# A 2-D real FFT filter pair with a gated mix: a new order list, with some steps on other engines

## The chip, the cores and the metric

The kernel runs on one core of a Trainium2 chip. The metric is the device time of one execution in microseconds, as the median of several runs. The core has five engines that each work through their own queue in order: TensorE (PE; its weight loads, PEld, overlap its matmuls), VectorE (DVE), ScalarE (ACT), GpSimd (POOL) and SyncE (SP), which here only issues transfers. They meet through semaphores.

## The reference

```python
def _A_ref(x, w_r, w_i):                 # _B_ref is the same
    B, S, D = x.shape                    # 1, 2048, 1024
    X = rfft2(x.astype(float32), axes=(-2, -1))
    X = X * (w_r + 1j * w_i)             # w_r, w_i: 2048 x 513
    return irfft2(X, s=(S, D), axes=(-2, -1)).astype(bfloat16)

x = A_x
g = sigmoid((x * gate_w).sum(-1, keepdims=True))
return g * _A_ref(x, A_w_r, A_w_i) + (1 - g) * _B_ref(x, B_w_r, B_w_i)
```

Both filters act on the same x (B_x is not used), so the forward transform is made once, the products and inverse transforms twice, and the gate mixes the two results row by row. All inputs are bfloat16.

## The kernel before

Every transform is a matmul with a constant matrix. Rows are split as 2048 = 128 × 16 (s2, s1), columns into four quarters, so that even and odd frequencies (parity e and o) can be treated apart. `ORDER` is one long list of tokens; the program executes the list in order, and each token emits its instructions on one engine. So each engine's queue is the order of its tokens, and nothing else is scheduled. The letter at the end of a token names the engine (A, D, P for ScalarE, VectorE, GpSimd), the digit at the end of a TensorE token its PSUM bank.

The stages, with their tokens:

- **Loading.** `x:S:s:n` loads n of the 16 blocks of x, `c` constants, `W:S:n` the weights of unit n (16 units: 0 to 7 even, 8 to 15 odd), all issued by SP except the F1 constants and the gate weights `gws` (ScalarE). At most eight transfers are in flight: each further issue waits for the eighth before it. `warm` runs eight matmuls on zeros, `tab` loads ScalarE's sigmoid table.
- **Column transform.** `F1:s1:par` (line 321) makes eight matmuls of 128 columns into one bank. Its two halves are added and subtracted into the tile y: either one half is copied out (`FC`) and VectorE folds the copy with the bank (`FD`, two instructions), or both halves are copied (`FX`) and GpSimd folds (`FP`). `pw` and `gc` prepare small weights on GpSimd.
- **Row transform.** For each unit, `F2` (four matmuls for each of two halves), its copy `T`, `F3` (12 matmuls with the twiddles WF and their negated imaginary part WN) and its copy `X`. `neg` makes WN from WF on ScalarE.
- **Products.** `P:n:r` (line 488) multiplies X with four weight planes, 128x2048 elements for each r, on VectorE; `Y` on TensorE, `NA` and `N` on VectorE patch one column of the product.
- **Inverse row transform.** `J` (32 matmuls) into two times two banks, its two copies `R` (128x1024 each) into a ring of five `rl` buffers, two stores `H` to a scratch in HBM. When all 16 stores of a parity have landed, `L:par:v` loads them back in another layout, eight loads of 512 KB: the even ones over x, the odd ones over weights.
- **Gate.** `GH`, `GC`, `GT`, `GK`, `GZ` form the gate from y, `GS` applies the sigmoid (two instructions), `GW` (line 436) multiplies the inverse matrix E with it into EA and subtracts that from E into EB, for four s1 at a time.
- **Inverse column transform and output.** `V` (eight matmuls with EA and EB, which also mixes the two filters) and its copy `VC`; then, for each v and s, matmuls with IG: `C` keeps the cosine and sine half apart (four matmuls of 256 columns), `U` gives their sum (four of 512). An even row is made from `C`: whole (`E`), or copied out and mixed on GpSimd (`EX`, `EQ`), or its sine half copied and both sums made on VectorE (`ES`, `EF`: in the code, unused). An odd row adds to and subtracts from the even row: on VectorE from PSUM (`OR`), or copied out (`OC`) and mixed by GpSimd (`OP`), or through a buffer (`QD`, `QP`). `S` stores the result.

The copies' scratch `tmp` is a rotation of eight tiles in wx, which later holds the weights of units 8 to 11.

Of the kernel before, what the change touches and what calls it, by code (L numbers as in the profile page):

```python
# [712 lines left out]
```

## Time and profile before

| | us |
|---|---|
| time, median of 3 runs | 117.29 (117.25 to 117.5) |
| span of the profiled execution | 115.6 |
| VectorE busy | 97.0 |
| TensorE busy | 103.6 |
| ScalarE busy | 84.4 |
| GpSimd busy | 46.2 |
| bytes moved, mean rate | 36.79 MB, 318 GB/s |

The span is what the page of the profile covers, from the first to the last instruction of one execution; the time also holds what lies around it. Busy TensorE time includes the drain of each matmul, so it is not TensorE at its peak. A row of a group names the line, the engine, the operation, output and input tile with their shapes, the count, and then busy time, mean length of one and idle time before it. A row of the chain of waits or of a timeline begins with its start and its length in microseconds.

### The profile page before, as it was taken

To read this page: it belongs to the slowest core of one execution; us is meant where nothing else is said; L and a number is where in the kernel's file an instruction comes from. 1 tells how busy PE (TensorE), PEld (TensorE's weight loads), DVE (VectorE), ACT (ScalarE), POOL (GpSimd) and SP (SyncE) were. 2 spreads that over 40 slices of the span, in tenths; PEclk is the share of its full clock that TensorE was granted. 3 is DMA by queue.
4 is the path that set the end of the run, shared out by engine and by line. 5 is a ranking of instruction groups with operands and counts; after the bars stand their busy time and mean duration, and the time that the engine had idled before them with its cause. 6 is when DMAs were issued, how large, how long until landed. Compare 5 with 4: busy or idle time off the path is not lost.

```text
span 115.6 us, 3953 instructions
## 1 busy us (share of the span) xinstructions
PE 103.6 (90%) x1619; PEld 71.3 (62%) x1619; DVE 97.0 (84%) x164; ACT 84.4 (73%) x138; POOL 46.2 (40%) x74
## 2 busy tenths in 40 slices
PE   5999999999999699898889899989979999999900
PEld 2499989875567256463445357459859765867400
DVE  0099999999999999999899999999157349999970
ACT  4009488999999999999999999977735844534300
POOL 1066995900000000000000000057986999999920
PEclk9999999999999999999999999999999999999995
DMA  3999999999579999669999999999999992482874
GB/s 90 348 326 401 403 374 367 363 397 408 210 222 324 371 394 373 169 263 397 350 293 354 348 306 401 254 357 382 352 353 411 403 418 98 198 346 119 327 279 181
DMA packets 17794, 36.79 MB, mean 318 GB/s; under 512 B 1904, under 2 KB 10736, under 8 KB 17776
## 3 DMA queue, kind: packets, MB, share of 16 engines
q1 hardware_dynamic: 17488, 36.44, 87.5%
q8 instruction: 12, 0.20, 0.6%
q10 hardware_dynamic: 288, 0.10, 0.4%
q14 instruction: 6, 0.05, 0.1%
HBM read 23.96 MB, written 12.58 MB: 316 GB/s over the span
## 4 chain that ended last, share of the span: by engine, by line
PE 39%; DVE 19%; DMA 16%; ACT 16%; issue 4%; SPq 1%; DVEq 1%; ACTq 0%
ACT rl L204 11%; PE ps L581 9%; PE ps L565 8%; DVE y L382 7%; PE ps L450 6%; PE ps L334 5%; DMA sc<-rl 5%; DMA re<-sc 4%; DMA ig<-cst_ig 4%; PE ps L537 3%; DMA re<-in_x_dram 3%; PE ps L480 3%; DVE p L494 3%; ACT X L204 3%; PE ps L590 3%
## 5 line engine op out<-in xcount | busy, mean ns | idle before, releaser
L615 POOL TENSOR_TENSOR re<-wx 128x256 f32<-128x256 f32 x28 | 19.6, 730 | 55.3 <-DMA re<-sc 53.1
L204 ACT CAST rl<-ps 128x1024 bf16<-128x1024 f32 x29 | 29.6, 1142 | 0.7 <-ACT wx L204 0.7
L204 ACT COPY wx<-ps 128x256 f32<-128x256 f32 (+1 forms) x39 | 17.2, 498 | 10.5 <-PE ps L334 8.2
L537 PE MATMUL ps<-p,wj 32*64 32x512 bf16 x512 | 20.5, 381 | 2.5 <-ACT rl L204 2.0
L204 ACT CAST V<-ps 128x512 bf16<-128x512 f32 x25 | 13.8, 601 | 11.3 <-PE ps L565 8.4
L494 DVE TENSOR_TENSOR p<-X,ro 128x2048 bf16<-128x2048 bf16 x16 | 19.1, 1215 | 0.0
L450 PE MATMUL ps<-fd,y 128*128 128x256 bf16 x128 | 16.5, 273 | 0.4 <-ACT rl L204 0.4
L382 DVE TENSOR_TENSOR y<-ps,wx 128x256 bf16<-128x256 f32 x48 | 16.4, 412 | 0.1
L334 PEld LDWEIGHTS <-re 128*128 128x128 bf16 x256 | 15.2, 100 | 1.6 <-DMA re<-in_x_dram 1.0
L334 PE MATMUL ps<-f,re 128*128 128x128 bf16 x256 | 15.8, 224 | 0.3
L204 ACT CAST T<-ps 128x512 bf16<-128x512 f32 x26 | 15.5, 693 | 0.0
L537 PEld LDWEIGHTS <-wj 32*64 32x64 bf16 x512 | 8.4, 103 | 10.6 <-issue 7.5
L382 POOL TENSOR_TENSOR y<-wx 128x256 bf16<-128x256 f32 x16 | 11.1, 734 | 8.2 <-DVE wx L206 5.9
L635 DVE TENSOR_TENSOR ot<-re,ps 128x512 bf16<-128x512 f32 x22 | 13.8, 681 | 0.4
L450 PEld LDWEIGHTS <-y 128*128 128x128 bf16 x128 | 11.5, 97 | 4.1 <-issue 2.6
L581 PE MATMUL ps<-ig,V 128*128 128x512 bf16 x56 | 13.4, 380 | 0.0
L204 ACT CAST X<-ps 128x1024 bf16<-128x1024 f32 x12 | 13.2, 1118 | 0.0
L206 DVE COPY wx<-ps 128x512 f32<-128x512 f32 (+1 forms) x10 | 5.8, 578 | 7.4 <-PE ps L334 4.8
L480 PE MATMUL ps<-T,wf 64*64 64x256 bf16 (+1 forms) x128 | 10.2, 332 | 1.1 <-DVE np L514 1.0
L590 PE MATMUL ps<-ig,V 128*128 128x256 bf16 x72 | 9.7, 273 | 0.0
L494 DVE TENSOR_TENSOR p<-X,wx 128x2048 bf16<-128x2048 bf16 x8 | 9.4, 1217 | 0.0
L494 DVE TENSOR_TENSOR p<-X,y 128x2048 bf16<-128x2048 bf16 x8 | 9.3, 1215 | 0.0
(60 smaller groups left out, 138.4 us busy)
## 6 DMA issues: line engine op xcount, KB each, us to landing
sc<-rl SPq DMA_DIRECT2D x32, 256.0 KB, 4.7
ro<-in_we_dram SPq DMA_DIRECT2D x8, 512.0 KB, 8.3
re<-sc SPq DMA_DIRECT2D x8, 512.0 KB, 6.1
ro<-sc SPq DMA_DIRECT2D x8, 512.0 KB, 7.7
re<-in_x_dram SPq DMA_DIRECT2D x7, 512.0 KB, 8.0
out_dram<-ot SPq DMA_DIRECT2D x7, 512.0 KB, 2.6
wx<-in_wo_dram SPq DMA_DIRECT2D x4, 512.0 KB, 6.6
y<-in_wo_dram SPq DMA_DIRECT2D x4, 512.0 KB, 5.0
```

What stands on the lines that cost most here:

```text
L204: nc.scalar.copy(out=out, in_=in_)
L334: nc.tensor.matmul(o, lhsT=lh, rhs=rh, start=(h == 0), stop=(h == 1))
L382: Q[e].tensor_tensor(yo[:, v, k:k + n, s1, :], a.rearrange("p (k c) -> p k c", c=4), b.rearrange("p (k c) -> p k c", c=4), op)
L450: nc.tensor.matmul(ps[:, v * 256:v * 256 + 256], lhsT=y[:, v, par, b, 2 * t:2 * t + 2, :, :].rearrange("p j s c -> p (j s c)"), rhs=C["FD" ...
L480: nc.tensor.matmul(view(ps[ho, tt * 512:(tt + 1) * 512], dst), lhsT=lh, rhs=view(T[hp(jh), tt, :], src), start=(w == 0), stop=(w == 1))
L494: nc.vector.tensor_tensor(p[:, r], xb, w, ALU.mult)
L537: nc.tensor.matmul(o, lhsT=lh, rhs=src[r, ri, wi, tt], start=(q == 0), stop=(q == 3))
L565: nc.tensor.matmul(ps[:, ch * 128:ch * 128 + 128], lhsT=RR[par][:, v, ch // 2, s, c0 + 256 * ab:c0 + 256 * ab + 128], rhs=Ew[:, s1, :], st ...
L581: nc.tensor.matmul(ps, lhsT=Vs[par, v][:, s, ch, :], rhs=rh, start=(ch == 0), stop=(ch == 3))
L590: nc.tensor.matmul(ps[:, o:o + 256], lhsT=Vs[par, v][:, s, ch, :], rhs=g[:, o:o + 256], start=(ch % 2 == 0), stop=(ch % 2 == 1))
L615: Q[e].tensor_tensor(EV[:, v, s, 256 * h:256 * h + 256], t[:, 0], t[:, 1], (ALU.add, ALU.subtract)[h])
L635: nc.vector.tensor_tensor(otile(v)[:, s, h, :], EV[:, v, s], PS["O", 1, v, s], (ALU.add, ALU.subtract)[h])
```

## The change

The order list is replaced. By tokens, before and after:

| | before | after |
|---|---|---|
| folds: `FD` VectorE / `FP` GpSimd / whole row `FG` | 24 / 8 / 0 | 20 / 11 / 1 |
| `T` on VectorE / ScalarE | 6 / 26 | 7 / 25 |
| `X` | 4 / 12 | 3 / 13 |
| `R` | 3 / 29 | 5 / 27 |
| `VC` | 7 / 25 | 4 / 28 |
| gate tiles `GW` (two instructions each) | 4 VectorE | 4 GpSimd |
| even rows whole / mixed by `EQ` / by `EF` | 2 / 14 / 0 | 0 / 6 / 10 |
| `EQ` on GpSimd / VectorE | 28 / 0 | 9 / 3 |
| odd rows as `U` / as `C` | 14 / 2 | 10 / 6 |
| `OR` / `OP` / `QD`, `QP` / `OF` | 22 / 6 / 4, 4 / 0 | 20 / 12 / 0 / 6 |
| result stores | 9 | 13 |

Other parts: x is loaded in another order of blocks (4, 10, 2, 8, 14, 6, 0, 1, 12) with `w0` second, and F1's blocks follow it; F1's constants are issued by ScalarE behind `gws` and `tab`; the constants FD, WF, WJ, PM come behind all of x, EZ, E and IG later. The negated twiddles are a third block of the constant WF, so `neg` and WN are gone and WF has 576 KB in its second load instead of 384. The sine copy of `ES` has a scratch tile of its own for each row, and a new pair does for odd rows what `ES` and `EF` do for even ones: `OS` copies the sine half, `OF` makes sum and difference on VectorE into a scratch tile, from which GpSimd's `OP` makes the two output halves.

```diff
-warm:8 c:A:F1 c:A:gws tab:A x:S:0:1 x:S:1:1 x:S:2:2 x:S:4:2 x:S:6:2 x:S:8:2 x:S:10:2 x:S:12:2 x:S:14:2 c:S:FD:0:1
-F1:1:o:0 F1:1:e:1 FX:1:o:D F1:0:o:2 FC:1:e:D F1:0:e:3 FP:1:o FD:1:e F1:3:o:0 F1:2:e:4 FC:0:e:D F1:3:e:1 gc:P FD:0:e
-F1:2:o:5 FC:3:e:A FC:2:e:D F1:4:e:3 FD:3:e FX:2:o:A F1:5:o:6 FX:0:o:A FD:2:e F1:5:e:5 FC:4:e:A FP:0:o FX:3:o:A FD:4:e
...
-OR:5:1:1 U:1:7:0:4 VC:1:7:1:A EQ:7:1:1:P OR:5:1:0 V:1:6:0:0 QP:3:1:1:P OR:7:0:0 S:S:5 U:1:7:1:1 VC:1:6:0:A OR:7:0:1
-VC:1:6:1:A QP:3:1:0:P U:1:6:0:0 S:S:7:0 OR:7:1:1 OR:7:1:0 U:1:6:1:2 QP:3:0:1:P OR:6:0:0 S:S:7:1 OR:6:1:1 OR:6:0:1
-S:S:3 OR:6:1:0 S:S:6
+warm:8 c:A:gws tab:A c:A:F1 x:S:4:2 c:S:w0 F1:5:e:1 x:S:10:2 F1:4:o:3 x:S:2:2 pw:P F1:10:o:6 F1:10:e:4 FC:5:e:A FD:5:e gc:P
+FC:4:o:A F1:11:o:2 FX:10:o:A x:S:8:2 FC:11:o:A F1:3:e:7 FP:10:o x:S:14:2 F1:11:e:5 FD:4:o F1:3:o:3 FX:10:e:D F1:4:e:1 x:S:6:2
+x:S:0:1 F1:2:e:6 FC:3:e:A FC:11:e:A FC:4:e:A F1:8:e:4 FX:3:o:A x:S:1:1 FD:11:o FP:10:e FD:11:e F1:9:o:5 FC:8:e:A FD:3:e
+F1:9:e:0 x:S:12:2 FX:2:e:A FD:4:e FC:9:e:A F1:8:o:7 c:S:WF:0:4 FC:9:o:A FP:3:o F1:14:e:2 FP:2:e F1:15:e:6 c:S:PM c:S:WJ:0:4
+c:S:FD:0:1 FC:8:o:A FX:14:e:A FD:8:e FD:9:e F1:7:e:3 FD:9:o F1:6:e:4 FC:6:e:A F1:0:e:5 FD:8:o F1:0:o:2 FP:14:e FD:6:e
+F1:1:e:7 F1:12:e:1 FC:7:e:A FX:15:e:A FC:0:e:A FX:1:e:A FD:7:e FD:0:e F1:2:o:6 F1:13:e:4 FP:15:e FC:12:e:A F1:12:o:0 F1:5:o:5
+FX:2:o:A FP:1:e FD:12:e FC:13:e:A F1:14:o:3 F1:15:o:6 FX:0:o:A FD:13:e F2:1:0:2 FC:5:o:A FX:14:o:A FC:15:o:A F2:1:1:1
+FC:12:o:D W:S:0 c:S:FD:1:2 T:1:0:A FD:5:o W:S:1 T:1:1:A FD:12:o F2:0:0:3 F1:13:o:7 T:0:0:A F2:0:1:5 F3:1:1 F2:2:1:3 FC:13:o:A
+FD:15:o T:0:1:A F3:0:5 X:1:A FP:2:o F2:2:0:4 W:S:3 c:S:WF:4:16 FD:13:o F2:3:0:2 T:2:1:D P:1:0 X:0:A Y:1:3 F2:3:1:7 NA:1:D
+T:3:0:A FG:1:o:6 T:3:1:A P:1:1 P:0:0 F1:6:o:3 W:S:5 W:S:2 T:2:0:A FY:1:o:A F3:3:0 c:S:EZ c:S:E FP:0:o FX:6:o:A Y:0:4 P:0:1
+X:3:A F1:7:o:7 FP:14:o FP:6:o NA:0:D F2:5:1:5 N:1:D T:5:1:A W:S:9 c:S:WJ:4:16 W:S:4 FC:7:o:D F2:5:0:6 N:0:D F3:2:2 FD:7:o
+T:5:0:A X:2:A F2:4:0:4 J:1:0:5 F2:4:1:7 Y:2:2 T:4:0:A GH:3 R:1:0:A R:1:1:A T:4:1:A P:3:0 GC:A J:0:5:0 W:S:11 P:2:0 Y:3:7
+NA:2:D W:S:7 F3:5:2 P:2:1 H:1:0 W:S:6 P:3:1 F2:6:0:4 NA:3:D N:2:D R:0:0:A GT:0:7 R:0:1:A X:5:D GT:3:7 N:3:D GT:1:7 GT:2:7
+P:5:0 F3:4:5 GK:A T:6:0:A X:4:A J:2:2:0 F2:6:1:7 Y:5:6 P:5:1 R:2:1:A H:0:1 H:1:1 H:2:1 GZ:0:4 T:6:1:A NA:5:D GS:0 R:2:0:D
+P:4:0 Y:4:6 F3:6:0 NA:4:D GZ:1:2 X:6:A GS:1 F2:7:0:4 F2:7:1:5 T:7:1:A P:4:1 T:7:0:D J:3:0:6 R:3:0:A R:3:1:D F2:8:1:2 F2:8:0:5
+Y:6:4 F3:7:0 N:4:D W:S:10 N:5:D T:8:1:A J:4:2:6 NA:6:D P:6:0 P:6:1 T:8:0:A X:7:A W:S:8 P:7:0 R:4:0:A W:S:15 H:3:0 H:2:0
+J:5:0:4 F2:9:1:3 F2:9:0:2 N:6:D T:9:1:D R:4:1:A T:9:0:D P:7:1 F3:8:6 R:5:0:A F2:11:0:3 R:5:1:A X:8:A H:3:1 J:6:4:0 P:8:0
+Y:7:6 NA:7:D H:4:0 W:S:12 W:S:13 F2:11:1:7 T:11:1:D T:11:0:A P:8:1 F3:9:2 R:6:0:A c:S:IG H:5:0 R:6:1:A F2:10:1:7 F3:11:5
+X:9:A H:4:1 H:5:1 T:10:1:A N:7:D W:S:14 J:8:0:3 F2:10:0:2 X:11:A P:9:0 H:6:1 R:8:0:D R:8:1:A F2:12:1:6 F2:12:0:7 P:11:0
+T:10:0:A H:0:0 T:12:1:A H:8:1 J:7:4:0 T:12:0:A R:7:0:A F3:10:2 P:9:1 J:9:6:4 R:7:1:A F2:13:0:0 R:9:0:A X:10:D R:9:1:A
+F2:14:1:2 F2:14:0:3 F3:12:6 H:6:0 P:11:1 P:10:0 F2:15:1:5 T:14:1:D T:14:0:A F2:13:1:1 P:10:1 X:12:A H:7:0 F3:14:2 T:15:1:A
+J:10:6:4 T:13:0:D T:13:1:A GW:P:4:4 H:8:0 P:12:0 X:14:A H:7:1 P:12:1 F3:13:0 R:10:0:A GW:P:0:4 L:0:3 F2:15:0:3 R:10:1:A
+X:13:A T:15:0:A L:0:1 V:0:3:1:2 J:11:6:4 VC:0:3:1:D P:14:0 L:0:4 L:0:6 L:0:0 H:9:0 V:0:1:1:1 V:0:3:0:0 P:14:1 R:11:0:A H:10:0
+L:0:2 VC:0:1:1:A VC:0:3:0:D P:13:0 R:11:1:A J:12:6:2 R:12:0:D R:12:1:A J:14:0:4 P:13:1 H:10:1 H:11:0 F3:15:2 X:15:D V:0:1:0:6
+GW:P:12:4 R:14:0:A C:0:3:1:7 V:0:0:1:1 P:15:0 R:14:1:A VC:0:1:0:A C:0:3:0:0 V:0:0:0:4 VC:0:0:1:A EX:3:0:A H:12:1 H:9:1
+J:13:2:5 GW:P:8:4 C:0:0:1:0 EX:3:1:D H:14:1 VC:0:0:0:A EQ:3:0:0:P H:11:1 C:0:0:0:4 V:0:2:1:7 R:13:0:A EX:0:1:D R:13:1:A
+EQ:3:0:1:P EX:0:0:D P:15:1 EQ:3:1:0:D C:0:1:1:1 EQ:0:0:1:D EX:1:1:A VC:0:2:1:D C:0:1:0:0 EX:1:0:A V:0:4:0:4 V:0:2:0:3
+J:15:5:1 L:0:5 VC:0:4:0:A H:12:0 V:0:5:1:4 VC:0:2:0:A EQ:3:1:1:P L:0:7 C:0:2:1:0 R:15:0:A EQ:0:0:0:P V:0:4:1:7 ES:2:1:A
+R:15:1:D EF:2:1 C:0:2:0:5 H:13:0 ES:2:0:D VC:0:5:1:A VC:0:4:1:A V:0:5:0:1 EQ:1:1:0:P EQ:0:1:0:P H:14:0 EF:2:0 H:13:1
+C:0:4:0:3 C:0:4:1:6 V:0:7:1:0 ES:4:1:D ES:4:0:A C:0:5:1:7 VC:0:5:0:A EQ:0:1:1:P EQ:1:1:1:P VC:0:7:1:A EQ:1:0:0:D ES:5:1:A
+EF:4:0 H:15:0 V:0:7:0:5 C:0:5:0:1 V:0:6:0:0 H:15:1 V:0:6:1:2 VC:0:7:0:A VC:0:6:0:A ES:5:0:A EQ:1:0:1:P VC:0:6:1:A C:0:7:0:5
+C:0:7:1:3 L:1:0 EF:5:1 EF:4:1 ES:7:1:A C:0:6:0:6 L:1:1 V:1:0:1:0 ES:7:0:D VC:1:0:1:A ES:6:0:A C:0:6:1:7 V:1:0:0:2 EF:5:0
+EF:7:1 EF:7:0 ES:6:1:A C:1:0:1:4 V:1:1:1:3 V:1:1:0:5 OS:0:1:A VC:1:1:1:A VC:1:0:0:D EF:6:0 L:1:3 U:1:0:0:0 L:1:2 VC:1:1:0:A
+L:1:6 V:1:3:1:3 OF:0:1 C:1:1:1:6 V:1:3:0:1 U:1:1:0:2 L:1:7 OR:0:0:0 OR:0:0:1 VC:1:3:1:A OS:1:1:A V:1:2:0:3 OF:1:1 OP:0:1:1
+V:1:2:1:4 VC:1:3:0:A VC:1:2:0:A OR:1:0:0 OR:1:0:1 C:1:3:1:0 VC:1:2:1:A V:1:7:1:1 OS:3:1:A EF:6:1 C:1:3:0:2 U:1:2:1:4 OP:0:1:0
+VC:1:7:1:A OF:3:1 OS:3:0:A C:1:7:1:3 OS:7:1:A OF:3:0 L:1:4 V:1:4:1:6 U:1:2:0:7 V:1:6:1:0 V:1:4:0:2 VC:1:4:1:A VC:1:4:0:A
+OR:2:1:0 OR:2:1:1 U:1:4:1:5 OP:1:1:1 L:1:5 OP:1:1:0 OP:3:1:0 S:S:0 OF:7:1 V:1:7:0:3 U:1:4:0:2 OP:3:1:1 OR:2:0:0 OR:2:0:1
+OP:3:0:1 OR:4:1:1 VC:1:6:1:A C:1:6:1:4 OP:3:0:0 OR:4:1:0 OR:4:0:1 OR:4:0:0 VC:1:7:0:A OP:7:1:1 V:1:6:0:0 OS:6:1:A U:1:7:0:1
+VC:1:6:0:A OP:7:1:0 OF:6:1 OR:7:0:0 V:1:5:0:3 S:S:1 VC:1:5:0:A OP:6:1:1 U:1:6:0:2 OP:6:1:0 S:S:2:0 V:1:5:1:4 S:S:2:1
+VC:1:5:1:A OR:7:0:1 S:S:3:0 S:S:3:1 U:1:5:0:0 U:1:5:1:1 OR:6:0:0 OR:6:0:1 OR:5:0:0 S:S:4:0 S:S:4:1 OR:5:0:1 S:S:7 OR:5:1:0
+S:S:6:0 OR:5:1:1 S:S:6:1 S:S:5:0 S:S:5:1
```

```diff
@@ -140,7 +137,7 @@
     G = np.concatenate([IG[:, 0], IG[:, 1], -IG[:, 1]], axis=-1)
     c["IG"] = _bf16np(G.transpose(2, 0, 1, 3))
     s1 = np.arange(NS1)
-    WF = np.zeros((128, NT, 2, 64))
+    WF = np.zeros((128, NT, 3, 64))
     WJ = np.zeros((128, NT, 12, NS1))
     for t in range(NT):
         for jh in range(2):
@@ -164,7 +161,7 @@
                 be[1, jj, :, p] = 1j * eps * w.conj()
             al = al.reshape(64, 64)
             h = slice(64 * jh, 64 * jh + 64)
-            WF[h, t, 0], WF[h, t, 1] = al.real, al.imag
+            WF[h, t, 0], WF[h, t, 1], WF[h, t, 2] = al.real, al.imag, -al.imag
             h = h if t % 2 == 0 else slice(64 - 64 * jh, 128 - 64 * jh)
             b = np.stack([be[:, p // 32, :, p] for p in range(64)])
             for cc in range(2):
@@ -225,7 +222,7 @@
     yo = y[:].rearrange("p v e b t s c -> p v (e b t) s c")
 
     C = {}
-    for n, sh, dt in (("F1", [3, 128], BF16), ("FD", [2, 2, 2, 256], BF16), ("WF", [NT, 2, 64], BF16), ("WN", [NT, 64], BF16), ("PM", [2, 2, 128], BF16),
+    for n, sh, dt in (("F1", [3, 128], BF16), ("FD", [2, 2, 2, 256], BF16), ("WF", [NT, 3, 64], BF16), ("PM", [2, 2, 128], BF16),
                       ("IG", [2, 2, 768], BF16), ("E", [128], BF16), ("EZ", [128], BF16),
                       ("WJ", [NT, 12 * NS1], BF16),
                       ("EA", [NS1, 128], BF16), ("EB", [NS1, 128], BF16), ("zt", [NS1], BF16), ("one", [1], BF16),
@@ -274,13 +271,6 @@
             w = yf[:, (n - 12) // 2, 0, (n % 2) * 2048:(n % 2) * 2048 + 2048]
         Ws[n] = w.rearrange("p (t a m) -> p t a m", t=2, a=4)
         Q[q].dma_start(w, w_in[n // NU][n % NU])
-
-    def neg(e, a, b):
-        s, t = C["WF"][:, int(a):int(b), 1], C["WN"][:, int(a):int(b)]
-        if e == "A":
-            nc.scalar.mul(t, s, -1.0)
-        else:
-            Q[e].tensor_scalar(t, s, -1.0, None, ALU.mult)
 
     def gate_coef(e):
         q = Q[e]
@@ -473,10 +463,7 @@
                         if g == 1:
                             return ap[:, o:o + ln]
                         return ap.rearrange("p (g m) -> p g m", g=2)[:, :, o:o + ln]
-                    if w == 2:
-                        lh = C["WN"][hp(jh), t, :]
-                    else:
-                        lh = C["WF"][hp(jh), t, w, :]
+                    lh = C["WF"][hp(jh), t, w, :]
                     nc.tensor.matmul(view(ps[ho, tt * 512:(tt + 1) * 512], dst), lhsT=lh, rhs=view(T[hp(jh), tt, :], src),
                                      start=(w == 0), stop=(w == 1))
 
@@ -595,14 +582,13 @@
 
     def even_sin(v, s, e):
         v, s = int(v), int(s)
-        if ("E", v) not in TM:
-            TM["E", v] = tmp()
-        cp(e, TM["E", v][:, s], PS["O", 0, v, s][:, 256:512])
+        TM["E", v, s] = tmp()
+        cp(e, TM["E", v, s][:, 0], PS["O", 0, v, s][:, 256:512])
 
     def even_sum(v, s):
         v, s = int(v), int(s)
         for h, op in enumerate((ALU.add, ALU.subtract)):
-            nc.vector.tensor_tensor(EV[:, v, s, 256 * h:256 * h + 256], PS["O", 0, v, s][:, 0:256], TM["E", v][:, s], op)
+            nc.vector.tensor_tensor(EV[:, v, s, 256 * h:256 * h + 256], PS["O", 0, v, s][:, 0:256], TM["E", v, s][:, 0], op)
 
     def even_parts(v, s, e):
         v, s = int(v), int(s)
@@ -634,6 +620,17 @@
         v, s, h = int(v), int(s), int(h)
         nc.vector.tensor_tensor(otile(v)[:, s, h, :], EV[:, v, s], PS["O", 1, v, s], (ALU.add, ALU.subtract)[h])
 
+    def odd_sin(v, s, e):
+        v, s = int(v), int(s)
+        TM["OS", v, s] = tmp()
+        cp(e, TM["OS", v, s][:, 0], PS["O", 1, v, s][:, 256:512])
+
+    def odd_fold(v, s):
+        v, s = int(v), int(s)
+        t = TM["O", v, s] = tmp()
+        for h, op in enumerate((ALU.add, ALU.subtract)):
+            nc.vector.tensor_tensor(t[:, h], PS["O", 1, v, s][:, 0:256], TM["OS", v, s][:, 0], op)
+
     def odd_mix(v, s, h):
 
         v, s, h = int(v), int(s), int(h)
@@ -651,10 +648,10 @@
         r = slice(0, 2) if s == "b" else slice(int(s), int(s) + 1)
         Q[q].dma_start(ov[:, 2 * v:2 * v + 2, :][:, r], OT[v][:, r].rearrange("p s h d -> p s (h d)"))
 
-    fn = dict(warm=warmup, x=load_x, c=load_c, W=load_w, neg=neg, gc=gate_coef, tab=table, pw=pair_weights,
+    fn = dict(warm=warmup, x=load_x, c=load_c, W=load_w, gc=gate_coef, tab=table, pw=pair_weights,
               F1=f1, FG=f1g, FY=f1y, FC=f1c, FD=f1d, FX=f1x, FP=f1p, GH=gate_hat, GC=gate_copy, GT=gate_turn, GK=gate_cols, GZ=gate_z, GS=gate_s, GW=gate_weights,
               F2=f2, T=f2c, F3=f3, X=f3c, P=prod, Y=parts, NA=patch_mul, N=patch, J=i1, R=i1c, H=scratch_store, L=scratch_load, V=i2, VC=i2c, U=i3, C=i3f,
-              E=even_out, ES=even_sin, EF=even_sum, EX=even_parts, EQ=even_mix, OC=odd_copy, OP=odd_pool, OR=odd_row, QD=odd_mix, QP=odd_out, S=store)
+              E=even_out, ES=even_sin, EF=even_sum, EX=even_parts, EQ=even_mix, OC=odd_copy, OP=odd_pool, OR=odd_row, OS=odd_sin, OF=odd_fold, QD=odd_mix, QP=odd_out, S=store)
     order = [tok.split(":") for tok in ORDER.split()]
     for t in order:
         fn[t[0]](*t[1:])

```

## The prediction

> **What bounds the kernel now.** I read the busy time by stage first, then the groups, the chain of waits and the timelines of single engines. An execution takes 117.29 us in the median of three (117.25 to 117.5); the profiled one spans 115.6 us. I hold the 1.69 us between them constant and make the sum on the span. About 0.2% (0.23 us) is what a measurement can tell from no change.
>
> Busy time by stage (PE, PEld, DVE, ACT, POOL, clock, DMA share, GB/s):
> ```profile
> 5.90:24.50 18.60, 18.39 (x299) 17.16 (x297) 18.42 (x53) 13.07 (x34) 14.14 (x31) 1.00 1.02 377
> 24.50:75.70 51.20, 47.39 (x935) 27.83 (x934) 50.22 (x68) 51.20 (x69) 0.00 (x0) 1.00 0.93 322
> 75.70:89.00 13.30, 12.21 (x175) 10.60 (x175) 9.40 (x14) 7.88 (x16) 10.35 (x15) 1.00 1.04 371
> 89.00:108.40 19.40, 19.40 (x194) 13.14 (x192) 15.03 (x25) 10.59 (x20) 19.40 (x23) 1.00 0.67 270
> ```
> Up to 75.7 us VectorE never rests, and from 24.5 on ScalarE doesn't either: what either gains or loses there moves the end. GpSimd does nothing at all in the 51.2 us of the products. Behind 89 us TensorE is full.
>
> Groups, with the mean ns of one:
> ```profile
> L494 DVE TENSOR_TENSOR p<-X,ro 128x2048 bf16<-128x2048 bf16 x16 | 19.1, 1215 | 0.0
> L382 DVE TENSOR_TENSOR y<-ps,wx 128x256 bf16<-128x256 f32 x48 | 16.4, 412 | 0.1
> L635 DVE TENSOR_TENSOR ot<-re,ps 128x512 bf16<-128x512 f32 x22 | 13.8, 681 | 0.4
> L631 POOL TENSOR_TENSOR ot<-re,wx 128x512 bf16<-128x512 f32 x6 | 7.6, 1278 | 0.0
> L439 DVE TENSOR_TENSOR ea<-ea,e 128x512 bf16<-128x512 bf16 x4 | 1.7, 414 | 0.0
> ```
> Instructions overlap at their ends, so I use the spacing, not the mean: product 1.135 us (four take 4.62), a fold's pair 0.68, T, V or wx copy 0.61, X or rl copy 1.14, patch pair 0.30, gate pair 0.79, odd row 0.634. On ScalarE a copy of 512 columns is 0.5, of 1024 columns 0.93.
>
> Start, and last stages (VectorE, SP and chain):
> ```profile
> 0.71 0.38 ACTq L264 DMA_DIRECT2D f<-cst_f  x1
> 1.64 1.28 ACT L299 ACT_TABLE_LOAD   x1 [1.64 <-PEq L693]
> 4.87 1.05 PE ps L334 x8
> ...
> 62.28 2.53 SPq L554 DMA_DIRECT2D re<-sc  x4
> 80.40 5.18 DMA re<-sc
> 83.95 4.47 SPq L554 DMA_DIRECT2D ro<-sc  x8
> 94.94 5.24 DVE L635 TENSOR_TENSOR ot<-re,ps 128x512 bf16<-128x512 f32 x8
> 103.12 8.93 DVE L635 TENSOR_TENSOR ot<-re,ps 128x512 bf16<-128x512 f32 x14
> ```
> VectorE idles between 80 and 94.9, then runs 27 instructions without a break to 112.05. The odd loads leave at 83.95, when the last H store has landed.
>
> **Step 1, the start: +0.2 us.** F1's constants are now issued behind gws, the table load (1.28) and its 0.21 us activation: near 2.65 instead of 0.71. They landed 3.2 us after issue; the second x load needed 3.7, and now five x loads are ahead, so 5.9 to 9 (a queue of 2.1 MB at 350 GB/s, in front). I take 6.4, near the rows, against 4.87. Then 28 F1 blocks of eight matmuls at 0.466 (64 in 3.73 us) 13.1; the first 1.5 us ran 7 matmuls per half microsecond instead of 13, 0.7; four F2 and an F1 block 2.3, T 0.6, F3 0.6, X 1.05. First product at 6.4 + 18.3 = 24.7; it was 24.53. VectorE has 19 folds ahead of it instead of 24, 3.4 us less, but PE's blocks come no sooner.
>
> The Trainium skill (TensorE: Matmul & The Clock Gate, Part 1) says the array runs at half rate until a window of about 3.4 us was busy, windows running free. The slices agree in kind (7, then 13 at 6.3 us). By it the new 1.6 us gap between warm-up and F1 may cost a second cold window, 1.7 us instead of 0.7: the sum would be 1.0 higher.
>
> **Step 2, the products: +3.8.** VectorE from the first product to the end of the last. Before: 32 products 36.3, patches 2.4, six T 3.6, four X 4.6, one rl 1.1, three gate pairs 2.4, gate column 0.15: 50.6, measured 51.2. After: 36.3, 2.4, six T 3.7, three X 3.4, four rl 4.6, a late copy and fold 1.0, two V 1.2, three even copies 1.8: 54.4, with the same 0.6 idle 55.0. ScalarE's queue over the same stretch is 55 before and after: negations (0.42 and 0.96) and two rl go, an X, GK, FY and copies for the even rows come. So the last product ends at 24.7 + 55.0 = 79.7 instead of 75.7.
>
> **Step 3, gate tiles on GpSimd: +3.5.** VectorE's 3.2 us for four pairs is gone (three counted above). Instead GpSimd gets eight operations of 128x512, nearest row 1278 ns, 1.25 spaced: 10.0 us. They depend on the sigmoid and E alone, so they start near 40 us wherever their tokens stand, while products run; GpSimd's time itself is hidden, nothing reads the tiles before 66. But products read both operands from memory on chip, and so do these. No row shows both at once. Bounds: 0 (folds, one operand in PSUM, took 410 to 425 ns with GpSimd busy or not) and 10.0 (every operation holds VectorE up). Products and patch sums are 37.7 of 54.4 us, 0.7; if either may have to wait, half the meetings fall on VectorE: 10.0 × 0.7 × 0.5 = 3.5. The fold row is of another kind, so I take the middle.
>
> The Trainium skill (SBUF — State Buffer, "Who interferes with whom") says a VectorE instruction with two SBUF inputs contends with a GpSimd instruction that reads SBUF, and that the one that starts second is blocked for the whole length of the other. No row of the trace before shows it. By it the price lies between 3.5 and 10, not at 0.
>
> **Step 4, first even load: +0.8.** L:0:3 waits for all 16 even stores; the last, H:7:1, has its rl copy near 59.2 by ScalarE's queue (X:1 at 23.6, then every entry at its spacing, 0.5 of waits). Stores landed in 4.3 to 5.0 there, the first load in 5.0: V:0:3:1 near 69.2, where VectorE's queue wants its copy near 67. Queued behind it: on TensorE J:11, for which ScalarE's R:11 waits, on VectorE product 14. Lower bound 0 (2.3 was the shortest store, 4.8 the shortest load), upper 2.2; I take 0.8, as fewer transfers are in flight. In the kernel before, V came 4 us behind its load.
>
> **Step 5, behind the last product: −5.45.** Before: 75.7 to VectorE's end at 112.05, 36.35, and 3.55 to the end of the span. After: J and the last rl copy 2.6, store issue 0.5 and landing 3.0 (2.3 to 4.7), odd load 4.4 (3.7 to 5.7; the even loads are now ahead of the last stores), so V:1:0 10.5 behind the product. From there VectorE: V and its copy 1.4 + 0.6, an even pair 0.68, then six OF pairs, one EF pair and 20 odd rows, 4.8 + 12.7, waits 0.8: 21.0. TensorE needs 18.9 (four U of 0.87 became C of 0.44, −1.7) and is not the bound. The ten EF pairs (6.8) cost nothing, as they lie in the gap between 80 and 94; without that gap they are on the path. GpSimd loses 19 EQ and four QP, gains six OP: 15 us of OP from the first OF pair, done before VectorE. Last store 256 KB instead of 512 (2.0 against 2.6): 2.95. Sum 10.5 + 21.0 + 2.95 = 34.45 against 39.9: −5.45.
>
> Span: 79.7 + 0.8 + 3.5 + 34.45 = 118.45; time 120.1.
>
> Loading the negated weights costs 0.26 MB, 0.7 us of DMA at 377 GB/s, in an SP queue that waits in W:S:11 for the late fold FD:7:o anyway: hidden. If not, 0.7 us. IG, EZ and E move back in that queue and land long before the first C and gate tile ask; W:S:11 holds W:S:7 and H:1:0, which products near 46 us and a ring of five buffers wait for: nothing, by these distances.
>
> **Rivals.**
> - No interference: step 3 costs nothing, 116.6. For it: the fold rows; against it: two operands each. Its spread, 115.4 to 117.9, crosses the old time. The same follows if the gate tiles run only when their tokens suggest, behind the products.
> - Faster: the odd stage decides. VectorE's first odd fold now comes 2.7 us behind the first odd V (1.4 + 0.6 + 0.68), where the first row came 5.9 behind it (89.06 to 94.94), and this is kept while steps 3 and 4 cost nothing and F1 lands by 5.9: 116.6 − 0.8 − 0.5 − 1.0 (store 2.3, load 4.1) = 114.3. It decides if the last product ends before 80. Against it: it needs three lower ends at once.
> - Start in the queue: F1's constants behind the x loads, PE at 8.7: +2.3, 122.4. For it: consts issued behind x loads needed 7 to 10 us; against it: they shared the x queue, F1 has its own.
> - Full blocking: 0.7 × 10.0 = 7.0 on VectorE, 123.6.
>
> **How the numbers follow.** Forecast with step 3 between 2 and 5: 0.44, 118.6 to 121.6. No interference 0.28, of which about half is under 117.06. Faster 0.12. Start 0.06. Full blocking 0.10. The range 115.2 to 123.2 leaves out most of full blocking and the better half of the faster case. Faster 0.12 + 0.17 + 0.02 = 0.31, same 0.05, slower 0.64.
>
> **What would show it.** Step 1: first F1 matmul near 6.4, first product near 24.7. Step 3: GpSimd's gate operations between 40 and 60 us, products or gate operations longer than 1.215 and 1.28 there; if both keep their lengths the step is wrong and the time is near 116.6. Step 4: VectorE idle before the copy of V:0:3:1. Step 5: VectorE from the first odd fold to its end in about 18 us. It is wrong as a whole if the last product ends near 80 us.

## The result and the profile after

The changed kernel took 122.87 us in the median of four runs (121.46 to 124.31), the kernel before 117.30 beside it. The ratio is 1.0343, with a 95% interval of 1.0305 to 1.0381: slower, by some 4 us. The four runs lie in two groups, near 121.5 (from which the ratio is taken) and near 124.3 (to which the profiled execution belongs), and what makes the 2.8 us between them is not shown. The terms below are those of the profiled execution, with a span of 122.5 and a time of 124.31.

Busy time by stage of the profile after, in the columns of the prediction (PE, PEld, DVE, ACT, POOL, clock, DMA share, GB/s): start, first product to end of the last, then to the first odd V, then the odd half.

```profile
5.90:22.70 16.80, 16.55 (x273) 15.12 (x272) 14.72 (x42) 13.73 (x33) 15.97 (x31) 1.00 1.03 400
22.70:85.70 63.00, 52.62 (x1015) 32.18 (x1013) 59.72 (x71) 52.66 (x71) 18.51 (x14) 0.95 0.83 289
85.70:97.50 11.80, 9.10 (x129) 7.24 (x128) 10.19 (x25) 8.24 (x18) 4.41 (x6) 1.00 0.77 273
97.50:116.60 19.10, 18.25 (x192) 12.86 (x190) 16.32 (x34) 10.96 (x23) 14.72 (x12) 1.00 0.82 318
```

The stretch of the products is 63.0 us long instead of 51.2. VectorE is busy for 59.7 of it; ScalarE, which before had no gap there, rests for 10 us; and the clock is no longer 1.00. Groups of the same profile (busy us, mean ns):

```profile
L481 DVE TENSOR_TENSOR p<-X,ro 128x2048 bf16<-128x2048 bf16 x16 | 22.4, 1435 | 0.0
L481 DVE TENSOR_TENSOR p<-X,y 128x2048 bf16<-128x2048 bf16 x8 | 9.6, 1224 | 0.0
L507 DVE TENSOR_TENSOR p<-np 128x16 bf16<-128x16 f32 x8 | 3.6, 467 | 0.0
L429 POOL TENSOR_TENSOR ea<-ea,e 128x512 bf16<-128x512 bf16 x4 | 6.6, 1640 | 11.3 <-ACT ea L424 11.3
L430 POOL TENSOR_TENSOR eb<-e,ea 128x512 bf16<-128x512 bf16 x4 | 6.3, 1584 | 0.3
```

The first sixteen products cost 3.3 us more than before (19.1); the last eight have their usual length. The patch sums doubled (1.8 before). Only some of these operations are stretched: four of the sixteen products and a few of the patch sums, beside GpSimd's gate operations, and two further patch sums (0.65 and 0.48, near 28 us) beside two of GpSimd's folds. Each operation can be seen in the timelines of VectorE and GpSimd (start, length, count):

```profile
40.12 2.09 DVE L481 TENSOR_TENSOR p<-X,ro 128x2048 bf16<-128x2048 bf16 x1
...
44.72 6.12 DVE L481 TENSOR_TENSOR p<-X,ro 128x2048 bf16<-128x2048 bf16 x3
50.76 1.17 DVE L507 TENSOR_TENSOR p<-np 128x16 bf16<-128x16 f32 x1
```

```profile
39.98 1.15 POOL L429 TENSOR_TENSOR ea<-ea,e 128x512 bf16<-128x512 bf16 x1 [11.29 <-ACT ea L424]
41.20 2.02 POOL L430 TENSOR_TENSOR eb<-e,ea 128x512 bf16<-128x512 bf16 x1
43.18 1.15 POOL L429 TENSOR_TENSOR ea<-ea,e 128x512 bf16<-128x512 bf16 x1
```

A product takes 2.09 instead of 1.22, three take 6.12 instead of 3.49, a patch sum 1.17 instead of 0.22. A gate operation takes 1.15 where it isn't held up and 2.0 to 2.1 where it is. Where VectorE runs copies from PSUM, at 43 us, neither is longer. What this does to TensorE is in the waits from 48 to 60 us and in the same stretch by 2 us each:

```profile
PE ps L440 <- DVE T L203: 4.3, 1, 4.3
```

```profile
48.00:50.00 2.00, 0.23 (x12) 0.10 (x1) 2.00 (x2) 2.00 (x3) 2.00 (x2) 1.00 0.46 121
50.00:52.00 2.00, 0.00 (x0) 0.00 (x0) 2.00 (x3) 0.26 (x1) 1.92 (x2) 0.63 0.95 385
52.00:54.00 2.00, 1.47 (x20) 0.70 (x27) 2.00 (x3) 0.42 (x1) 1.07 (x1) 0.50 1.07 284
54.00:56.00 2.00, 2.00 (x38) 0.80 (x23) 1.53 (x3) 0.72 (x2) 0.00 (x0) 0.50 0.95 341
56.00:58.00 2.00, 2.00 (x23) 0.75 (x24) 1.51 (x2) 1.82 (x3) 0.00 (x0) 0.67 1.09 408
```

TensorE waits 4.3 us for one T copy behind the stretched products. The pause runs from 48.2 to 52.5 us. The clock falls to 0.50 at 50.5, still within the pause, and stays there until 57.3. ScalarE, with nothing to copy, is idle for most of 50 to 56, and VectorE in its turn has gaps from 55 on.

Start and later stages (timelines of ScalarE, SP and TensorE):

```profile
1.15 1.28 ACT L289 ACT_TABLE_LOAD   x1 [1.15 <-PEq L690]
1.21 0.39 ACTq L261 DMA_DIRECT2D f<-cst_f  x1
...
69.00 2.50 SPq L541 DMA_DIRECT2D re<-sc  x5
72.63 0.23 PE L552 MATMUL ps<-ea,re 128*128 128x128 bf16 x1 [2.05 <-DMA re<-sc]
...
93.82 3.77 SPq L541 DMA_DIRECT2D ro<-sc  x8
97.36 0.23 PE L552 MATMUL ps<-ea,ro 128*128 128x128 bf16 x1 [1.27 <-DMA ro<-sc]
```

The F1 constants leave at 1.21, while the table is loading. The first even load leaves at 69.0, the odd ones at 93.82 instead of 83.95.

### The profile page after: what moved, and what is told of

It reads as the page before. It is cut to its first block, busy times and chain, and to the rows that moved or that the text cites. A ratio compares the mean times of both kernels' runs of the same rounds, so it can differ in the third digit from the quotient of the medians.

```text
span 122.5 us, 3985 instructions
## 1 busy us (share of the span) xinstructions
PE 101.9 (83%) x1619; PEld 69.6 (57%) x1619; DVE 103.9 (85%) x172; ACT 87.1 (71%) x144; POOL 55.0 (45%) x71
## 4 chain that ended last, share of the span: by engine, by line
PE 37%; DMA 26%; DVE 21%; issue 7%; ACT 3%; SPq 3%; DVEq 1%; ACTq 0%
DMA sc<-rl 14%; DVE p L481 11%; PE ps L324 10%; DMA ro<-sc 7%; PE ps L440 7%; DMA re<-in_x_dram 5%; PE ps L568 5%; PE ps L467 4%; PE ps L524 4%; DVE rl L203 4%; PE ps L552 3%; SPq L541 2%; DVE p L507 2%; DVE ot L621 2%; DVE T L203 2%
## 5 line engine op out<-in xcount | busy, mean ns | idle before, releaser
L201 ACT CAST rl<-ps 128x1024 bf16<-128x1024 f32 x27 | 26.4, 1032 | 5.0 <-PE ps L524 3.9
L201 ACT CAST V<-ps 128x512 bf16<-128x512 f32 x28 | 16.1, 594 | 10.7 <-PE ps L552 4.8
L481 DVE TENSOR_TENSOR p<-X,ro 128x2048 bf16<-128x2048 bf16 x16 | 22.4, 1435 | 0.0
L601 POOL TENSOR_TENSOR re<-wx 128x256 f32<-128x256 f32 x9 | 7.8, 891 | 29.3 <-ACT wx L201 29.3
L617 POOL TENSOR_TENSOR ot<-re,wx 128x512 bf16<-128x512 f32 x12 | 14.9, 1275 | 11.8 <-issue 10.9
L372 DVE TENSOR_TENSOR y<-ps,wx 128x256 bf16<-128x256 f32 x40 | 14.0, 416 | 6.6 <-ACT wx L201 6.5
L372 POOL TENSOR_TENSOR y<-wx 128x256 bf16<-128x256 f32 x22 | 16.3, 775 | 4.3 <-ACT wx L201 4.3
L324 PEld LDWEIGHTS <-re 128*128 128x128 bf16 x248 | 14.6, 100 | 1.7 <-DMA re<-in_x_dram 1.2
L577 PE MATMUL ps<-ig,V 128*128 128x256 bf16 x88 | 12.6, 273 | 1.1 <-ACT V L201 1.1
L552 PE MATMUL ps<-ea,re 128*128 128x128 bf16 x64 | 8.6, 220 | 3.8 <-DMA re<-sc 3.1
L429 POOL TENSOR_TENSOR ea<-ea,e 128x512 bf16<-128x512 bf16 x4 | 6.6, 1640 | 11.3 <-ACT ea L424 11.3
L552 PEld LDWEIGHTS <-re 128*128 128x128 bf16 x128 | 7.9, 98 | 5.4 <-DMA re<-sc 4.4
L467 PE MATMUL ps<-T,wf 64*64 64x256 bf16 (+1 forms) x192 | 10.5, 324 | 0.3 <-DVE T L203 0.2
```

What stands on the lines that cost most here:

```text
L201: nc.scalar.copy(out=out, in_=in_)
L324: nc.tensor.matmul(o, lhsT=lh, rhs=rh, start=(h == 0), stop=(h == 1))
L372: Q[e].tensor_tensor(yo[:, v, k:k + n, s1, :], a.rearrange("p (k c) -> p k c", c=4), b.rearrange("p (k c) -> p k c", c=4), op)
L467: nc.tensor.matmul(view(ps[ho, tt * 512:(tt + 1) * 512], dst), lhsT=lh, rhs=view(T[hp(jh), tt, :], src), start=(w == 0), stop=(w == 1))
L481: nc.vector.tensor_tensor(p[:, r], xb, w, ALU.mult)
L552: nc.tensor.matmul(ps[:, ch * 128:ch * 128 + 128], lhsT=RR[par][:, v, ch // 2, s, c0 + 256 * ab:c0 + 256 * ab + 128], rhs=Ew[:, s1, :], st ...
```

## The experiments

Ratios are to the kernel before, measured on the same chip, with 95% intervals.

**Gate tiles, undone and done alone.** First the changed kernel with its gate on VectorE, then the old kernel with only its gate moved:

```diff
-GW:P:4:4 ... GW:P:0:4 ... GW:P:12:4 ... GW:P:8:4
+GW:D:4:4 ... GW:D:0:4 ... GW:D:12:4 ... GW:D:8:4
```

> The changed kernel with its four gate tokens on VectorE at the same places of the list (nothing else changed). Theory (blocking: a GpSimd operation that reads on-chip memory and a VectorE operation with both operands there exclude each other): VectorE gets 3.2 us of gate work back, but loses the 4.5 us by which its products and patch sums were longer between 40 and 53 us, and TensorE's 4.3 us pause with the half clock behind it goes: 118.0 to 120.0 us, products all near 1.22 us. Rival (GpSimd does no harm; the changed order itself is the cause): 3.2 us more on a full VectorE, 124 to 125.

```diff
-GW:D:4 GW:D:0 GW:D:12 GW:D:8
+GW:P:4 GW:P:0 GW:P:12 GW:P:8
```

> The kernel before with its four gate tokens on GpSimd, nothing else changed: this part of the change alone. Theory (blocking): VectorE saves 3.2 us and loses 4 to 5 where products and patch sums meet the eight operations, and more if TensorE pauses: 118 to 122. Rival (no interference): 114 to 117, products unchanged at 1.215 us.

The old kernel lost as expected: 119.17 us, 1.0182 (1.0105 to 1.0259), although 2.4 us of gate work left VectorE's products. Here TensorE made no such pause, and its clock was 1.00 throughout the products. What remains is the stretch itself: the first sixteen products took 22.0 us instead of 19.1 and the patch sums 3.4 instead of 1.8, together 4.5 us more. Less the 2.4 that left, this makes 2.1, which is the measured loss (1.8% of 117.15).

```profile
L494 DVE TENSOR_TENSOR p<-X,ro 128x2048 bf16<-128x2048 bf16 x16 | 22.0, 1394 | 0.0
```

The changed kernel gained nothing: 121.69, 1.0384 (1.0316 to 1.0453). There neither theory held. Its products are 1.22 us again and the clock is 1.00, but the stretch is still 60.8 us:

```profile
22.60:83.40 60.80, 50.84 (x1015) 32.02 (x1013) 58.82 (x79) 53.47 (x73) 6.62 (x6) 1.00 0.92 317
```

VectorE now does the gate itself (4.3 us with two operations that met GpSimd's even sums, at 0.95 and 0.83 instead of 0.42), and is busy for 58.8 of the 60.8 us. Most of this list's loss therefore lies elsewhere. What the gate on GpSimd costs here is less clear. The ratio of the changed kernel, 1.0343, is no higher than this one, but the same list with only F1's load moved (the experiment on the start, below) came out at 1.0538. So it is between nothing and about 1.5%.

**Reading or only writing.** Eight extra GpSimd operations in the old kernel, behind a small add that waits for the gate column; nothing uses what they write.

```diff
+        for _ in range(int(n)):
+            q.tensor_tensor(t[:, 512:1024], t[:, 0:512], t[:, 0:512], ALU.add)
```

> The kernel before plus eight useless GpSimd additions of 128x512 bfloat16 (and a small one ahead) on a tile that nothing else reads, right behind the gate column, that is from about 36 us on, amid the products. They leave the result as it is. Theory (blocking): VectorE loses 0.5 to 1.0 us for each, 121 to 125; the additions or the products beside them take near 2.1 us. Rival (no interference): 117.2 to 117.6.

```diff
+        for _ in range(int(n)):
+            q.memset(t[:], 0.0)
```

> The same as the additions, but eight GpSimd memsets of 128x1024 bfloat16, which write and read nothing. Theory in the form that only reads exclude each other: 117.2 to 117.7, products at 1.215 us. Rival (any GpSimd work amid products slows VectorE): as with the additions, 120 and more.

The adds cost 1.0472 (1.0384 to 1.0561), the memsets 1.0033 (0.9988 to 1.0077), which is nothing measurable. VectorE's timeline beside the adds, and beside the memsets:

```profile
39.81 1.15 DVE L441 TENSOR_TENSOR eb<-e,ea 128x512 bf16<-128x512 bf16 x1
40.88 1.25 DVE L440 TENSOR_TENSOR ea<-ea,e 128x512 bf16<-128x512 bf16 x1
42.17 1.14 DVE L441 TENSOR_TENSOR eb<-e,ea 128x512 bf16<-128x512 bf16 x1
43.24 1.06 DVE L521 TENSOR_TENSOR p<-np 128x16 bf16<-128x16 f32 x1
```

```profile
39.86 0.42 DVE L440 TENSOR_TENSOR eb<-e,ea 128x512 bf16<-128x512 bf16 x1
40.21 0.42 DVE L439 TENSOR_TENSOR ea<-ea,e 128x512 bf16<-128x512 bf16 x1
```

Eight memsets ran from 37.88 for 8.01 us beside products and gate operations of the usual length. With the adds VectorE's two-operand work took up to three times as long, and here too TensorE paused, for 4.4 us from 40.0 on, and its clock was 0.50 from 41.6 to 48.4 us. So it is GpSimd's reads that VectorE waits for.

**One suspect at a time, on the list with its gate on VectorE.** The five even copies to ScalarE; IG's load at its old place; V:0:3:1 behind J:11:

```diff
-VC:0:3:1:D ... VC:0:3:0:D ... EX:3:1:D ... EX:0:1:D EX:0:0:D
+VC:0:3:1:A ... VC:0:3:0:A ... EX:3:1:A ... EX:0:1:A EX:0:0:A
```

> Base: the changed kernel with its gate tiles on VectorE (121.7 us, span 119.7). Edit: the five copies for even rows that the new list puts on VectorE ahead of the last product (V:0:3's two, EX:3:1, EX:0:1, EX:0:0) go to ScalarE. Theory A (the sum of VectorE's work ahead of the last product sets its end, step 2): 5 x 0.6 = 3.1 us leave that queue, the last product ends near 80.5 instead of 83.4 and the time is 118.5 to 120. Rival B (ScalarE, which is 53.5 of 60.8 us busy there, takes the wait over: rl copies and so the stores come later by as much): 121 to 122.5, with VectorE's idle time before the last product up from 2 to about 5 us.

```diff
-P:2:1 H:1:0 W:S:6 ... R:6:0:A c:S:IG H:5:0
+P:2:1 H:1:0 c:S:IG W:S:6 ... R:6:0:A H:5:0
```

> Same base (121.7). Edit: the load of the inverse table IG goes back to where the old list had it, behind the store H:1:0. Theory A (768 KB in the middle of the even stores make them land late, 4 to 9 us behind issue, and hold the ring of rl buffers and so ScalarE for 1.25 us): the wait of ScalarE on a store is gone, the first even load leaves 1 to 2 us before 64.25, VectorE's 0.8 us wait for V:0:3:1 goes, time 120 to 121.2. Rival B (the queue waits for the rl copies, not for bandwidth): load within 0.5 us of 64.25, time 121.4 to 122.

```diff
-V:0:3:1:2 J:11:6:4 VC:0:3:1:D P:14:0 ... H:9:0 V:0:1:1:1
+J:11:6:4 P:14:0 ... H:9:0 V:0:3:1:2 V:0:1:1:1 ... VC:0:3:1:D VC:0:3:0:D
```

> Same base (121.7). Edit: V:0:3:1 stands behind J:11 on TensorE and its copy one product later on VectorE. Theory A (step 4: what is queued behind the load's wait is delayed by it): the 2.4 us wait of TensorE and the 0.8 us of VectorE no longer stand ahead of J:11 and product 14; the last product ends about 0.8 earlier, 120.6 to 121.2. Rival B (the wait only comes back one place later, at V or at an rl copy): 121.5 to 122.

The copies, IG and V gave 1.0304 (1.0234 to 1.0373), 1.0252 (1.0169 to 1.0335) and 1.0288 (1.0207 to 1.037). Each interval overlaps that of the base, so none is shown to help alone. With the copies on ScalarE the last product ended at 83.7 (base 83.4), since VectorE now waited for TensorE instead, as rival B had it:

```profile
62.96 0.69 DVE L203 CAST T<-ps 128x512 bf16<-128x512 f32 x1 [1.99 <-PE ps L440]
66.66 0.69 DVE L203 CAST T<-ps 128x512 bf16<-128x512 f32 x1 [1.88 <-PE ps L467]
```

With IG early the first even load left 0.8 us sooner (63.44) and VectorE's wait for V went. The last product ended at 83.2, but in this profile the first product had begun 1.3 us later than in the base (23.94 against 22.64, F1 having run slowly until 9.0 us), so the stretch between them was 1.5 us shorter: 59.3 against 60.8. Counted from the first product, the load too left 2.1 us sooner, which is what theory A asked; but no gain in time is shown beyond the intervals. With V later the last product ended at 82.1 (the profiled execution took 120.02).

**Together.** Copies and IG, and around the last product two even sums to GpSimd and one V copy to ScalarE; then also the last J and its copies right behind the last product, two stores earlier, and V later:

```diff
-EQ:3:1:0:D ... EQ:0:0:1:D ... VC:0:2:1:D
+EQ:3:1:0:P ... EQ:0:0:1:P ... VC:0:2:1:A
```

> Same base (121.7). Edit: the five copies on ScalarE, IG early, and around the last product two even sums to GpSimd and V:0:2:1's copy to ScalarE, so that the last rl copy follows its J at once. Theory A (VectorE's work ahead of the last product, and the chain last product, rl copy, store, odd load behind it, set the end): last product near 79.5, last rl copy within 2 us of it, 2 us less in front of the odd loads, time 116 to 118. Rival B (TensorE and VectorE behind the first odd V are the bound, whatever comes before): 119 to 121, with VectorE's end as far as 21.7 us or more behind the first odd V.

```diff
-P:15:1 EQ:3:1:0:P C:0:1:1:1 EQ:0:0:1:P EX:1:1:A VC:0:2:1:A C:0:1:0:0 EX:1:0:A V:0:4:0:4 V:0:2:0:3 J:15:5:1 ... R:15:0:A ... R:15:1:D
+P:15:1 C:0:1:0:0 V:0:2:0:3 J:15:5:1 R:15:1:D EQ:3:1:0:P EQ:0:0:1:P VC:0:2:1:A R:15:0:A EX:1:0:A V:0:4:0:4 C:0:1:1:1 EX:1:1:A
```

> Base: the kernel with the copies on ScalarE and IG early (119.0 us, span 117.3, last product's end 79.6, last rl copies at 82.65 and 82.63, the first odd V's copy at 93.2). Edits: J:15 and its two copies stand right behind the last product, the stores H:9:1 and H:11:1 go ahead of H:12:1 (the last copy waited 3.1 us for the buffer that H:11:1 frees), and V:0:3:1 stands behind J:11. Theory A (the chain last product, J, copy, store, odd load sets the end once the product is early): copies end near 82, odd loads leave near 86.5 instead of 88.5, time 117.0 +- 0.8, which is no slower than before. Rival B (what is taken from that chain is given back in the odd stage, whose TensorE and VectorE work lies behind even rows that now come later): odd loads leave 2 us earlier, but VectorE's end moves less than 0.7 and the time is 118.3 to 119.3.

The first gave 118.99 us, 1.0132 (1.0051 to 1.0212): clearly under the base, 1 us above what theory A asked and at the lower edge of rival B's 119 to 121. The last product ended at 79.6, with VectorE busy for 56.4 of 57.0 us. The second gave 119.03, 1.0131 (1.0051 to 1.0211): the odd loads left at 86.57 instead of 88.53, as A said, and the time did not move, as B said. (The profiled execution took 117.88.) This second list is the mended one of what follows.

**The gate on GpSimd in that list.** The tokens of the first diff, reversed.

> The same kernel with its eight gate operations on GpSimd again, at the same tokens. Theory A (step 3: GpSimd's operations hold up products for about 4.5 us and VectorE's own operations would take 3.2): last product 1 to 2 us later than with the gate on VectorE, time 0.5 to 2.5 us longer. Rival B (the move is a gain where the list is not otherwise disturbed): time shorter by 1 us or more.

It gave 124.36 us, 1.0519 (1.0414 to 1.0624), against 1.0131: 4.5 us (3.8% of 117.5), though VectorE has four pairs less to do. That is nearly twice theory A's most (2.5). Stages of 4 us without and with the gate on GpSimd:

```profile
50.00:54.00 4.00, 3.30 (x66) 2.01 (x63) 4.00 (x7) 4.00 (x6) 0.00 (x0) 1.00 1.02 343
```

```profile
50.00:54.00 4.00, 0.23 (x6) 0.23 (x3) 4.00 (x5) 2.00 (x3) 3.92 (x3) 1.00 0.94 257
54.00:58.00 4.00, 3.72 (x55) 1.54 (x54) 4.00 (x5) 2.69 (x4) 2.46 (x2) 0.64 0.91 341
58.00:62.00 4.00, 3.63 (x48) 1.36 (x47) 2.67 (x4) 2.43 (x3) 0.00 (x0) 0.51 0.42 143
```

TensorE pauses (3.8 us, from 50.1 on), its clock is 0.50 from 55.1 to 61.9, and VectorE is short of work from 58 to 62. The two profiles, with spans of 116.1 and 123.6, differ in three places. First, with the gate on GpSimd the first product came 2.24 us later (24.86 against 22.62), long before any gate operation ran. TensorE waited 1.48 us for a block of x, up to 7.73 us, and its clock was 0.50 from 7.3 to 10.7:

```profile
L325 PE MATMUL ps<-f,re 128*128 128x128 bf16 x248 | 16.1, 229 | 2.3 <-DMA re<-in_x_dram 1.5
```

Second, the stretch of the products is 2.7 us longer (59.46 against 56.76). VectorE is busy for as long as before, 56.15 against 56.05 us: what the blocking adds makes up for the gate work that left. The 2.7 us are waits. Third, the work behind the last product is 2.6 us longer, and the last rl copy there waits 3.8 us for a store instead of 1.1. So what the gate on GpSimd adds in this trace is waits; whether the longer one at the end is its doing too isn't shown. Whether the other runs also began late isn't shown; if they did, up to 2.2 of the 4.5 us belong to the start and not to the gate.

**The start.** F1's load first in ScalarE's queue of the changed kernel.

```diff
-c:A:gws tab:A c:A:F1 x:S:4:2
+c:A:F1 c:A:gws tab:A x:S:4:2
```

> The changed kernel whole, with the load of F1's constants as the first entry of ScalarE's queue, as in the old list. Theory A (the table load doesn't hold the transfer: in the changed kernel it left at 1.21 us, during the load): first F1 matmul at 4.8 instead of 5.16, first product 0 to 0.4 earlier, time within 0.5 us of the changed kernel's 121.5. Rival B (step 1: the place in that queue is worth about 1.5 us): first matmul unchanged or 1 us earlier with the time 1 us or more shorter.

The first F1 matmul came at 4.92 instead of 5.16, but the first product at 23.13, 0.43 us later than in the changed kernel and not 0 to 0.4 earlier, as A asked. The time was 123.45 (1.0538, 1.0457 to 1.0619), not within 0.5 us of 121.5. So the place isn't worth 1.5 us, as rival B had it, but A's figures for the product and the time weren't met either, and why is not settled.

**The new end alone.** The old list up to the last even load, without the negations, then five even rows by sine copy and pair on VectorE, and from the odd loads on the changed kernel's list.

```diff
-EX:2:1:D ... EQ:2:1:0:P ... E:3:0:D ... U:1:0:0:1 ... OC:0:0:A
+ES:2:1:A EF:2:1 ... EX:3:0:A ... C:1:0:1:4 ... OS:0:1:A OF:0:1
```

> The old list as it stands up to the last even load (gate tiles on VectorE at their old places, old start, old copies), without the negations (negated weights loaded), and from there the new end: rows 2, 4, 5, 6 and 7 of the even half by a sine copy and a pair on VectorE, then the changed kernel's list from its odd loads on, word for word (span 115.6 and time 117.3 for the old end). Theory A (step 5: the new end is a gain by itself, 2 to 3 us as measured in the changed kernel's own end, and what the change loses it loses ahead of the last product): last product near 75.5 as in the old list, odd loads at 83.5 to 84.5, VectorE's end 21 to 22 us behind the first odd V, span 113 to 114.2, time 114.7 to 115.9. Rival B (the new end only pays for itself where the list ahead of it left ScalarE and VectorE idle; here its sine copies and pairs delay the odd loads or V): time 116.8 or more.

It gave 117.16 us, 0.9979 (0.9946 to 1.0012): the same as before. Theory A fell. The odd loads did leave at 83.60 (old list 83.95), but the even rows were not further than in the old list:

```profile
87.32 0.23 PE L554 MATMUL ps<-ea,re 128*128 128x128 bf16 x1 [2.31 <-DMA re<-sc]
```

TensorE still waited for the last even loads at 87 us (2.3 us, against 0.8 in the old list between 80 and 95), with even rows to do before the odd ones. (The profiled execution took 119.5 us, and its times behind this point aren't used.) No kernel tried here is shown to be faster than the one before.

## Why the prediction came out as it did

The forecast was slower, 120.1 us, through VectorE's longer stretch of products and GpSimd's interference, against a gain at the end. The sign and these two causes were right. On the span it had 118.45 us against 122.5, the sum of three errors: −2.0 at the start, +3.7 in the products, +2.35 behind them. The first hid a third of the other two, so that the total came out as near as it did is in part luck.

- **Step 1, the start (24.7 forecast, 22.70 measured): wrong in sign.** It held F1's transfer back behind the table load. The transfer left at 1.21 us and the first matmul ran at 5.16. The other 0.8 us is the sum of 18.3, which was 17.5: in the old kernel VectorE's 32 fold instructions without a break ended just as the first product began, so that five folds fewer brought it forward is likely, though no run tried it alone. The estimate from the Trainium skill (TensorE: Matmul & The Clock Gate, Part 1), a second cold window, wasn't put to the test here: the gap that was to cause it was 0.40 us instead of 1.6, and from 6.3 us on F1 ran 13 matmuls in half a microsecond, as before. Elsewhere the start does vary: with the gate on GpSimd in the mended list, the clock was 0.50 for 3.4 us from within a wait of 1.48 us on, and the first product came at 24.86.
- **Step 2, VectorE's count: right.** 54.4 us of work was forecast. VectorE is busy for 59.7, of which about 4.8 is what the gate operations added (0.9 and 2.6 on products, 1.3 on patch sums), so 54.9.
- **Step 3, gate on GpSimd: right in mechanism, its 3.5 us too small.** VectorE's operations grew by about 4.8, near the middle of the bounds of 0 and 10 and 1.3 above the term. What the step lacked is what comes next: TensorE's 4.3 us pause, the half clock, and 1.2 us of waits of VectorE for T and the patches, where 0.6 of idle time was counted. With the 1.1 us of step 4 and the 0.5 of step 2, these make up most of the +3.7. The Trainium skill (SBUF — State Buffer, "Who interferes with whom") says that a two-input VectorE instruction contends with GpSimd's reads and not with an instruction that only writes; the adds and memsets agree (1.0472 and 1.0033). Its block for the whole length of the other was to cost between 3.5 and 10 us. The 4.8 lies there, since the waits fall on both sides: four of the eight GpSimd operations grew by 0.9 to 1.0, and on VectorE four products and a patch sum by about 0.9 each.
- **Step 4, the first even load: 1.9 against 0.8.** It counted ScalarE's queue with 0.5 us of waits. ScalarE stood still for TensorE, and the load left at 69.0; with the gate on VectorE it left at 64.25 and the wait was 0.8. This forecast thus came true without the pause, which it did not foresee.
- **Step 5, behind the last product: 36.8 against 34.45.** Product to first odd V 11.6 (10.5 forecast: the last copy stood behind two even sums and a V copy, and the store took 4.38, not 3.0), V to VectorE's end 22.0 (21.0), the last store 3.2 (2.95). The gain of 3.1 us against before is real as a number, but the list with the old products and the new end shows what it is: with the even half no further than in the old list, the new end gains nothing measurable. The shorter end was bought with the even V, copies and sums that step 2 counts ahead of the last product. On this reading steps 2 and 5 are one move, and the prediction counted its return as a saving of its own; no run undid the even work alone. VectorE's time from its first odd fold to its end was 19.2 us, where about 18 was forecast.

Of the 3.4%, then: the end alone gives nothing, so the loss most likely lies ahead of the odd loads. There the gate on GpSimd costs 1.8% in the old list, up to 3.8% in the mended one and between nothing and 1.5% in the changed one, where VectorE's own gate work and waits for loads come in its place. The mid-stage copies, IG's place and the work around the last product are 2.5% together. The remaining 1.3% (0.5 to 2.1) was not taken apart by a run. The profile of the first of the two lists under "Together" (span 117.3) at least places it: against the old kernel the start is 1.9 us shorter, the stretch of the products 5.8 longer (57.0 against 51.2, with VectorE busy for 56.4 against 50.2) and what follows 2.2 shorter.

The rivals: "no interference" fell with the lengths; "faster" with the last product's end at 85.7, not before 80; "start in the queue" with the first matmul at 5.16. "Full blocking" had the right place and too high a price, 7.0 us against 4.8. That its 123.6 us lies near the measured time is luck, since TensorE's pause wasn't in it.

## What to carry to other kernels

Before work is moved to an idle engine, ask what it reads while the busy engine works: on this chip eight GpSimd operations that read cost a VectorE full of two-operand work more than doing them itself (in the old list 4.5 us of longer operations for 2.4 us saved), and eight that only write cost nothing measurable. Follow a delay one engine further than the one that is held up: behind a pause of some 4 us TensorE also ran at half its clock for 6.8 us. And when a stage gets shorter because part of its work now runs earlier, test the new stage behind the old front: it may gain nothing by itself.

## What the runs showed of the hardware

- A pause of about 4 us in TensorE's work went with a granted clock of 0.50 for 6.8 us, in three traces: the changed kernel (4.3 us of pause), the old one with the adds (4.4) and the mended list with the gate on GpSimd (3.8). The clock fell 2.3 and 1.6 us into the pause in the first two and 1.3 us behind its end in the third. The Trainium skill (TensorE: Matmul & The Clock Gate, Part 1) says that the array falls back to half rate after an idle window of about 3.4 us; the traces agree that it falls, but in two of them it fell sooner than that. At the start of the third trace the clock was 0.50 for 3.4 us, from about 1 us into a wait of 1.48 us on.
- At the start the column of granted clock read 1.00 while F1 ran 7 matmuls in half a microsecond instead of 13: this slow beginning is seen in the counts only.
- A transfer issued by ScalarE went out 0.06 us after its table load had begun; the load, 1.28 us long, didn't hold it.
